# A new hand-written order of issue for the attention block of a fused attention, RWKV and convolution kernel

## Chip, cores and metric

The kernel runs on one core of one Trainium2 chip. The metric is the device time of one execution in microseconds (us), the median of three runs. The core has TensorE (matmul, with its weight loads), VectorE, ScalarE, GpSimd, and SyncE, which issues most DMAs; each engine works through its own instructions in program order.

## Reference

Batch 2, 12 heads, 448 tokens, 64 numbers per head. Causal attention is followed by two feed-forward blocks:

```
scores = q @ k.T / 8, masked above the diagonal;  attn = softmax(scores);  x = attn @ v      # to (2, 448, 768)
xk = mu_k*x + (1-mu_k)*x_prev;  xr = mu_r*x + (1-mu_r)*x_prev                                # x_prev: one token earlier
r = sigmoid(xr @ w_r);  v = relu(xk @ w_k)**2 @ w_v;  x = r * v                              # w_r 768x768, w_k 768x1024
h = relu(x @ w_in);  gate = sigmoid(conv over 3 tokens of h);  out = (h * gate) @ w_out
```

The weights come as 64-bit floats and are turned into 32-bit ones on the chip.

## The kernel before, in words

Attention is cut into 12 **jobs**, one for each batch entry and pair of heads (job 6 to 11 are batch entry 1). The rows of a job's score matrix are cut into 7 tiles (0 to 6) of 64 tokens; tile i has 64·(i+1) columns, and both heads of the pair lie side by side on the 128 partitions. A job goes through these steps, which the program names by short words:

- `Lk`, `Lv`: DMA loads of q, k and v. `kqT`: TensorE transposes q and k; `kC.k`, `kC.q`: the copies out of PSUM.
- `sc.1`, `sc.2`: the score matmuls. `red.i`: VectorE adds the mask and takes the row maximum of tile i (L334). `exp.i`: ScalarE's exponential with its row sum (L343). `rec`: VectorE takes the reciprocals of the seven sums (L350, L351). `norm.i`: tile i is scaled in place (L71 on GpSimd, L73 on VectorE, L75 on ScalarE).
- `T.a` (tiles 6, 5, 0), `T.b` (tiles 4 to 1): TensorE transposes the scaled tiles. `C.aX`, `C.aY`, `C.bX`, `C.bY`: the four copies out of PSUM into the tile `pt`. `V.a`, `V.b`: the matmuls with v, into the tile `po`.
- `mP.1`, `mD.1`: the two passes that make xr of this pair of heads from `po`; `mP.0`, `mD.0` those for xk (L73 or L75, and L416). `mH`, `mL`: xr is split into a high and a low part for the three-matmul products (L82, L90); `mH`, `mL` of jobs 0 to 5 belong to batch entry 0.

Around the jobs stand steps of the first feed-forward block. `wN:L` loads a slice of weights (w0 to w5 are the six slices wr0 to wr5 of w_r, w6 to w8 the slices wk0 to wk2 of w_k); `a` (ScalarE), `b`, `c`, `d`, `e` turn it into 32-bit numbers (L136, L139, L141, L143, L145), and `h`, `l` split it into a high and a low part (L86, L90). `kN:H`, `kN:L` do the same for xk of job N. `prE.B.C` is one product step: three matmuls (L65 to L67) of weight slice E with chunk C (one pair of heads) of xr for batch entry B; so `pr4.1.0` is the first step that reads wr4. `srE.B` copies a finished sum out of PSUM. `E0` to `E3` are the first four sums with w_k, 18 matmuls each. `W*n` are matmuls on a constant that only keep TensorE at work.

All of these, on four engines, are issued in the order of one long string, `ORDER`, inside a scheduling region that keeps the order of issue on each engine as written. A token such as `8:norm.4/v` is job 8, step norm, tile 4, on VectorE; `/p` is GpSimd and `/a` ScalarE. So the string decides two things: where a step stands in its engine's queue, and, for the steps that more than one engine can do, which engine does it. PSUM banks and buffers go round in the order of the string too.

```
    with tc.manual_schedule(engines={ET.PE, ET.Activation, ET.DVE, ET.Pool}):
        for token in ORDER.split():
            issue(token)
```

Behind the string comes the rest of the program (the other sums with w_k, then w_v, w_in and w_out), whose order a scheduler sets. Its first TensorE instruction is the first matmul with wk2.

Of the kernel before, what the change touches and what calls it, by code (L numbers as in the profile page):

```python
# [19 lines left out]
def kernel(  # L20
# [451 lines left out]
    class Slice:  # L472
# [27 lines left out]
        3:kC.q/a 1:exp.5 0:C.bX/a 2:red.2 0:norm.5/p 1:rec 0:C.bY/a 1:norm.6/p 2:exp.2 2:red.1 0:T.a 1:norm.0/p  # L500
        2:exp.1 1:norm.5/p 0:C.aX/v 0:C.aY/v 2:red.0 1:norm.1/p 1:norm.4/p W*1 4:kqT 2:exp.6 4:kC.q/v 3:sc.2 2:exp.4
        2:exp.3 2:red.5 2:exp.0 W*1 1:T.a 3:red.3 0:V.a 5:Lk 1:norm.2/p Wend 2:exp.5 2:Lv 1:C.aX/v 3:red.2
        1:norm.3/p 4:kC.k/a 3:red.0 3:red.5 3:sc.1 2:rec 1:C.aY/v 2:norm.5/p 3:red.6 1:T.b 3:exp.0 3:red.4
        2:norm.0/p 3:exp.5 4:sc.2 3:red.1 3:exp.2 2:norm.6/p 6:Lk 4:red.3 0:V.b 1:C.bX/v 5:kqT w1:L 3:exp.3 3:exp.6
        2:norm.1/p 3:exp.4 4:red.2 1:C.bY/a 2:norm.4/p 2:norm.3/p 4:red.0 3:exp.1 4:red.5 2:T.a 2:C.aY/v 4:exp.0
        2:norm.2/p 5:kC.q/a 5:kC.k/a 2:T.b 3:Lv 2:C.aX/a 3:rec 0:mP.1/v 4:exp.5 3:norm.2/p 4:sc.1 4:exp.2 4:exp.3
        2:C.bX/v 3:norm.5/p 6:kqT 4:red.6 3:norm.1/p 5:sc.2 4:red.4 4:red.1 2:C.bY/v 4:exp.6 6:kC.k/a 2:V.a
        3:norm.4/p 4:exp.1 4:exp.4 0:mP.0/v 5:red.0 3:norm.3/p 5:red.3 w1:a 5:red.2 2:V.b 6:kC.q/v 3:T.b 3:norm.6/p
        7:Lk 3:norm.0/p 5:red.5 4:rec 3:T.a 3:C.bY/v w1:b/p 3:C.bX/a 4:norm.4/p 5:sc.1 1:Lv 2:mP.1/a 5:exp.0
        3:C.aX/v 2:mP.0/a 0:mD.1 5:red.1 5:red.6 4:norm.2/p 3:C.aY/a 0:mD.0 4:norm.3/p 3:V.b 5:exp.2 8:Lk 4:norm.5/p  # L510
        5:exp.3 6:sc.2 5:exp.1 4:norm.1/p 2:mD.1 4:norm.6/p 5:exp.5 5:red.4 7:kqT 7:kC.k/a 4:Lv 3:V.a 6:red.0 2:mD.0
        2:mH/p 4:norm.0/p 7:kC.q/v 3:mP.1/v 4:T.b 5:exp.6 9:Lk w1:c 0:mH/p 5:exp.4 5:rec 4:T.a 4:C.aX/a w1:d 1:V.a
        1:V.b 0:mL/p 6:exp.0 5:Lv 4:C.bX/a 3:mP.0/a 5:norm.5/p 5:norm.6/p 6:sc.1 6:red.5 6:red.3 4:C.bY/a 5:norm.0/p
        7:sc.1 4:C.aY/a 6:red.2 5:T.a 3:mD.1 6:exp.5 6:red.4 6:exp.2 6:red.1 6:red.6 4:V.a 7:red.1 6:exp.4 6:exp.3
        6:exp.1 6:exp.6 4:V.b 3:mD.0 5:C.aY/v 7:red.4 7:red.6 5:C.aX/a 8:kqT w2:L 1:mP.1/a 5:norm.3/p 6:rec
        5:norm.4/p 8:kC.k/a w1:e 2:mL/p 5:norm.2/p 6:Lv 5:norm.1/p 3:mH/p 5:T.b 8:kC.q/a 5:C.bY/a 7:sc.2 3:mL/p
        9:kqT w1:h 5:V.a 4:mP.1/v 1:mP.0/a 5:C.bX/v 7:red.2 9:kC.k/v 7:red.0 6:norm.3/p 7:exp.2 10:Lk 1:mD.1 7:exp.0
        6:norm.1/p 9:kC.q/a 5:V.b 7:red.3 6:norm.2/p 6:norm.4/p 7:exp.1 6:T.b 7:red.5 7:exp.3 w1:l/p 1:mD.0 1:mH/p
        6:norm.0/p 1:mL/p 6:C.bX/a 9:sc.1 4:mP.0/a 6:C.bY/v 9:red.6 8:sc.2 8:sc.1 6:norm.6/p 7:exp.4 4:mD.1 8:red.2
        6:norm.5/p w2:a 7:exp.6 8:red.3 11:Lk pr1.0.0 8:Lv pr1.0.1 4:mD.0 5:mP.1/v 7:exp.5 8:exp.3 w2:b/p 8:red.6  # L520
        7:rec 4:mH/p 8:red.1 5:mP.0/v 6:T.a 6:C.aY/a pr1.0.2 8:red.5 pr1.0.3 10:kqT 6:C.aX/a 8:exp.2 5:mD.1 6:V.a
        8:exp.6 8:red.0 6:V.b w2:c 8:exp.5 8:red.4 8:exp.1 7:norm.2/p 7:norm.0/p 10:kC.q/a 5:mD.0 10:kC.k/a 9:sc.2
        9:red.4 7:norm.6/p 9:red.1 8:exp.4 7:norm.3/p 11:kqT 7:norm.1/p 4:mL/v 8:exp.0 7:norm.4/p 7:T.b 5:mH/p w2:d
        5:mL/p 8:rec 7:norm.5/p 11:kC.q/v pr1.0.4 9:red.3 6:mP.1/a pr1.0.5 7:C.bY/a 8:norm.1/p 8:norm.3/p 6:mP.0/a
        9:red.2 11:kC.k/a 7:T.a 10:sc.1 sr1.0/v 7:C.bX/a w2:e 9:exp.4 8:norm.6/p 9:red.0 7:C.aX/a 7:C.aY/v 9:exp.2
        8:norm.2/p w2:h 10:sc.2 10:red.6 9:exp.0 9:exp.1 7:Lv w3:L 8:norm.0/p 9:exp.3 6:mD.1 7:V.b 9:red.5 9:exp.6
        7:V.a 8:norm.4/p 8:norm.5/p 10:red.5 10:red.0 9:exp.5 w3:a 10:Lv 6:mD.0 10:red.4 9:rec 8:T.b 7:mP.1/v 8:T.a
        w2:l/p 8:C.aX/a 8:C.bY/a w3:b/v 6:mH/p 10:exp.4 10:exp.0 8:C.aY/a pr2.0.0 7:mP.0/a 10:exp.5 9:norm.4/v w3:c
        10:red.3 9:norm.3/p pr2.0.1 pr2.0.2 pr2.0.3 10:red.2 pr2.0.4 w3:d 9:norm.0/p 8:C.bX/a pr2.0.5 11:sc.2
        10:red.1 7:mD.1 10:exp.6 w3:e 9:norm.5/p 11:red.5 7:mD.0 6:mL/p 11:Lv 10:exp.1 9:norm.2/v 11:sc.1 11:red.6  # L530
        9:Lv w3:h 8:V.b 9:norm.6/p 10:exp.3 8:V.a 11:red.2 sr2.0/a 9:T.a 11:red.3 w0:L 10:exp.2 8:mP.1/v 10:rec
        11:red.0 11:exp.6 w5:L 11:exp.0 9:norm.1/p w3:l/p 11:red.4 10:norm.3/v 9:T.b 11:exp.4 11:red.1 9:C.aY/v
        10:norm.0/p 11:exp.5 8:mP.0/v 11:exp.3 10:norm.1/p 10:norm.6/p pr2.1.0 9:C.bX/v pr3.0.0 pr3.0.1 10:norm.5/p
        9:C.aX/v 11:exp.2 11:exp.1 9:C.bY/a 7:mH/p pr3.0.2 11:rec pr3.0.3 10:norm.2/v 8:mD.1 11:norm.3/v 10:norm.4/p
        pr3.0.4 pr3.0.5 8:mD.0 w0:a 11:norm.5/a 10:T.a 10:T.b 10:C.aX/a 9:V.a 9:V.b w0:b/p 10:C.bY/v 11:norm.2/a
        11:norm.4/a 10:C.bX/v 11:norm.1/v 11:T.b 11:norm.6/p 11:norm.0/p 11:T.a 10:C.aY/a 11:C.bX/a w0:c w5:a
        11:C.bY/a 7:mL/p 9:mP.1/v 10:V.b 11:C.aX/a 10:V.a 9:mP.0/v 11:C.aY/a 9:mD.1 11:V.b 8:mH/p w0:d w5:b/v w0:e
        10:mP.1/a 11:V.a pr1.1.0 9:mH/a 10:mP.0/a pr3.1.0 8:mL/p 11:mP.1/v w0:h w0:l/p w5:c pr3.1.1 act2 10:mD.1
        w4:L 11:mP.0/a 11:mD.1 pr3.1.2 pr1.1.1 9:mD.0 pr0.0.0 9:mL/p 11:mH/p w5:d k5:H/p 10:mH/a pr0.0.1 w4:a
# [248 lines left out]
```

## Time and profile before

| | us |
|---|---|
| median of 3 runs | 365.78 (365.63 to 366.27) |
| the profiled execution, its own time | 365.75 |
| span of that execution, first to last instruction | 364.0 |
| TensorE busy in the span | 354.6 (97%) |
| VectorE busy | 289.0 (79%) |
| ScalarE busy | 222.1 (61%) |
| GpSimd busy | 112.0 (31%) |

Times below are us from the start of the span. A busy share is an average over stages with different limits, and a matmul counts as busy while it is in the pipeline, so the stages have to be looked at one by one. TensorE's granted clock is 1.00, the upper of its two levels (2.4 GHz), in every stretch of the rows below.

### The profile page before, as it was taken

What the parts mean: (1) busy time and instruction counts of PE and PEld (TensorE: products, weight loads), DVE (VectorE), ACT (ScalarE), POOL (GpSimd) and SP (SyncE); (2) the same over time, 40 slices, a digit from 0 to 9 for tenths busy, and PEclk for the clock granted to TensorE, in tenths of its full rate; (3) what the DMA queues carried; (4) which work ended last, traced back from release to release, by engine and by line L of the source; (5) the groups of instructions that cost most, each with busy time, mean ns of one, the idle gap of its engine ahead of it and who ended that gap; (6) DMA issues with size and microseconds to landing.
All of it is one profiled execution on the core that took longest, in us unless ns stands there. A gap on an engine that the chain in (4) does not pass through costs nothing.

```text
span 364.0 us, 7204 instructions
## 1 busy us (share of the span) xinstructions
PE 354.6 (97%) x2724; PEld 316.8 (87%) x2724; DVE 289.0 (79%) x551; ACT 222.1 (61%) x474; POOL 112.0 (31%) x168
## 2 busy tenths in 40 slices
...
GB/s 128 150 134 209 131 210 198 43 163 2 89 86 128 55 165 175 143 145 204 184 135 121 157 127 173 133 140 162 86 89 97 76 3 0 2 60 92 62 48 44
DMA packets 60351, 41.39 MB, mean 114 GB/s; under 512 B 34424, under 2 KB 59292, under 8 KB 60316
## 3 DMA queue, kind: packets, MB, share of 16 engines
...
q8 instruction: 21, 0.34, 0.4%
...
HBM read 38.17 MB, written 2.75 MB: 112 GB/s over the span
## 4 chain that ended last, share of the span: by engine, by line
PE 81%; DVE 16%; issue 2%; POOL 0%; ACT 0%; ACTq 0%; POOLq 0%
PE pk L66 5%; PE pk L67 5%; PE pout L67 5%; PE pk L65 5%; PE ph L67 5%; PE ph L66 5%; PE pout L66 5%; PE pout L65 5%; PE pv L66 5%; PE pv L67 5%; PE ph L65 5%; PE pv L65 5%; DVE e L334 5%; PE pr L65 3%; PE pr L66 3%; PE pr L67 3%
## 5 line engine op out<-in xcount | busy, mean ns | idle before, releaser
L724 POOL TENSOR_TENSOR cv<-cv,hT 128x448 f32<-128x448 f32 x16 | 23.2, 1454 | 153.1 <-ACT cv L723 153.1
L71 POOL TENSOR_SCALAR p<-p,st 128x64 f32<-128x64 f32 (+6 forms) x75 | 39.5, 548 | 20.5 <-ACT p L343 10.6
L343 ACT ACTIVATE p<-e,st 128x448 f32<-128x448 f32 (+6 forms) x84 | 42.0, 504 | 5.0 <-DVE st L334 4.7
L334 DVE CUSTOM_DVE_ANT_0 e<-s,mask 128x256 f32<-128x256 f32 (+6 forms) x84 | 31.8, 414 | 0.7 <-PE s L321 0.7
L753 ACT ACTIVATE osb<-pout 128x384 f32<-128x384 f32 x14 | 6.9, 492 | 40.9 <-PE pout L67 39.8
L391 PE MATMUL po<-pt,v 128*64 128x128 f32 (+4 forms) x384 | 24.2, 277 | 0.6 <-PE Ya L363 0.3
L321 PE MATMUL s<-kT,qT 64*64 64x64 f32 (+6 forms) x336 | 23.4, 388 | 0.4 <-DVE small L139 0.2
L391 PEld LDWEIGHTS po<-pt,v 128*64 128x64 f32 x384 | 20.3, 137 | 3.9 <-ACT p L343 0.5
L321 PEld LDWEIGHTS s<-kT,qT 64*64 64x64 f32 x336 | 14.7, 132 | 7.2 <-ACT qT L78 0.6
L65 PE MATMUL pout<-wo_t,g 128*128 128x384 f32 x49 | 16.4, 334 | 0.0
L66 PE MATMUL pout<-wo_t,g 128*128 128x384 f32 x49 | 16.4, 334 | 0.0
L67 PE MATMUL pout<-wo_t,g 128*128 128x384 f32 x49 | 16.4, 334 | 0.0
L343 ACT ACTIVATION_READ_ACCUMULATOR p<-e,st 128x1 f32 x84 | 16.1, 192 | 0.0
L65 PE MATMUL pout<-wo_u,g 128*128 128x384 f32 x42 | 14.0, 334 | 0.0
L66 PE MATMUL pout<-wo_u,g 128*128 128x384 f32 x42 | 14.0, 334 | 0.0
L67 PE MATMUL pout<-wo_u,g 128*128 128x384 f32 x42 | 14.0, 334 | 0.0
L720 DVE SCALAR_TENSOR_TENSOR cv<-hT,cw,cv 128x448 f32<-128x448 f32 x16 | 13.7, 855 | 0.1
L86 ACT ACTIVATE g<-cv 128x448 fp32r<-128x448 f32 x16 | 9.2, 576 | 7.1 <-POOL cv L724 7.0
L90 DVE TENSOR_TENSOR g<-cv,g 128x448 fp32r<-128x448 f32 x16 | 12.1, 755 | 1.8 <-ACT g L86 1.8
L719 DVE SCALAR_TENSOR_TENSOR cv<-hT,cw,cv 128x448 f32<-128x448 f32 x16 | 12.9, 810 | 0.0
L718 ACT ACTIVATE cv<-hT,cw 128x448 f32<-128x448 f32 x16 | 10.6, 670 | 2.3 <-DVE g L90 2.1
L90 POOL TENSOR_TENSOR xr<-m,xr 128x448 fp32r<-128x448 f32 x9 | 11.3, 1257 | 0.3
...
## 6 DMA issues: line engine op xcount, KB each, us to landing
rqk<-in_q_dram SPq DMA_DIRECT2D x24, 112.0 KB, 3.0
...
rqk<-in_k_dram SPq DMA_DIRECT2D x22, 112.0 KB, 2.9
...
```

What stands on the lines that cost most here:

```text
L65: nc.tensor.matmul(ps_out, lh, rh, start=first, stop=False)
L66: nc.tensor.matmul(ps_out, lh, rl, start=False, stop=False)
L67: nc.tensor.matmul(ps_out, ll, rh, start=False, stop=last)
L71: nc.gpsimd.tensor_scalar(out_, in_, s, 1.0, ALU.mult, ALU.mult)
L90: e.tensor_tensor(out_, x, f32(h), ALU.subtract)
L321: nc.tensor.matmul(held[self.name(f"s{f}")][1][h, o:z], qT[r, i * LO:(i + 1) * LO], kT[r, :(i + 1) * LO], start=True, stop=True,)
L334: nc.vector.tensor_tensor_reduce(t[:, :w], used(self.name(f"s{f}"))[:, o:z], mask[:, S - w:], -SCALE, 3e38, ALU.add, ALU.min, self.st[:, 0 ...
L343: nc.scalar.activation(p[:, :w], self.s[i][:, :w], AF.Exp, bias=self.st[:, 0, i:i + 1], scale=-1.0, accum_out=self.st[:, 1, i:i + 1],)
L391: nc.tensor.matmul(self.T["po"][j * D:(j + 1) * D, 1 + i * LO - z:1 + (i + n) * LO], self.v[:, kc, j], self.T["pt"][:, a - z:a + n * LO], ...
L719: nc.vector.scalar_tensor_tensor(a, hc, cw[:, NF + f:NF + f + 1], a, ALU.mult, ALU.add)
L720: nc.vector.scalar_tensor_tensor(a, hT[:, 2:S + 2], cw[:, 2 * NF + f:2 * NF + f + 1], a, ALU.mult, ALU.add)
L724: nc.gpsimd.tensor_tensor(a, a, hc, ALU.mult)
```

## The change

The string `ORDER` is replaced by another one. Nothing else differs. Of its 716 tokens 712 remain: the four that go are `W*n` tokens, of which there are now three fewer matmuls (14 instead of 17). All the other steps are there in both, in other places, and some on another engine. Two lines of the table:

```diff
-        0:Lk sm:L 1:Lk sm:a W0 W*2 0:kqT 0:kC.k/v sm:n 0:kC.q/a W*2 0:sc.1 2:Lk W*1 1:kqT 0:red.1 0:exp.1 0:red.4
+        0:Lk W0 sm:L W*2 0:kqT 0:kC.k/a sm:a 1:Lk 0:kC.q/v W*2 0:sc.2 W*1 1:kqT sm:n 0:red.0 0:red.5 0:red.2 0:red.3
```

Steps on each engine in the string, before and after: VectorE 220 and 223, ScalarE 175 and 183, GpSimd 115 and 104. The largest moves between engines are in `kC` (9 and 11 on VectorE), `C` (19 on VectorE in both), `mH` (10 and 7 on GpSimd), `norm` (75 and 70 on GpSimd), `kN:L` (6 and 3 on GpSimd), `l` of the weight slices (5 and 3 on GpSimd) and `b` (4 and 6 on GpSimd).

The first place is VectorE's queue behind the last `rec`, that of job 11. Before, from the last pass over a tile `p` (`norm.1` of job 11) on; `wr0c` and `wr5c` are slices being turned into 32-bit numbers, `m` and `mixed` the passes that make xr and xk:

```order
L73 TENSOR_SCALAR p_1_120<-p_1_120,st 128x128
L141 TENSOR_SCALAR wr0c<-wr0c 128x768
L73 TENSOR_SCALAR m_1904<-po_1836,mu 128x448
L73 TENSOR_SCALAR mixed<-po_1836,mu 128x448
L416 SCALAR_TENSOR_TENSOR m_1904<-po_1836,mu,m_1904 128x448
L143 SCALAR_TENSOR_TENSOR wr0c<-wr0raw,wr0c 128x768
L139 TENSOR_SCALAR wr5c<-wr5c 128x768
L145 SCALAR_TENSOR_TENSOR wr0c<-wr0raw,wr0c 128x768
```

and now, from the same pass on:

```order
L73 TENSOR_SCALAR p_1_120<-p_1_120,st 128x128
L78 COPY pt_135<-Xb_1829 128x512
L78 COPY pt_135<-Xa_1811 128x512
L78 COPY pt_136<-Xb_1876 128x512
L78 COPY pt_136<-Ya_1900 128x512
L78 COPY pt_136<-Yb_1877 128x512
L141 TENSOR_SCALAR wr4c<-wr4c 128x768
L416 SCALAR_TENSOR_TENSOR m_1917<-po_1855,mu,m_1917 128x448
L143 SCALAR_TENSOR_TENSOR wr4c<-wr4raw,wr4c 128x768
```

Slice wr0 has moved ahead of this place, three of the four last copies into `pt` have come to VectorE from ScalarE, and wr4 follows directly.

The second place is the end of the same queue's work on wr4. Before, the passes ahead of the low part of wr4 (`wr4hl`) were:

```order
L139 TENSOR_SCALAR wr4c<-wr4c 128x768
L141 TENSOR_SCALAR wr4c<-wr4c 128x768
L145 SCALAR_TENSOR_TENSOR wr5c<-wr5raw,wr5c 128x768
L416 SCALAR_TENSOR_TENSOR mixed<-po_1927,mu,mixed 128x448
L143 SCALAR_TENSOR_TENSOR wr4c<-wr4raw,wr4c 128x768
L90 TENSOR_TENSOR wr5hl<-wr5c,wr5hl 128x768
L145 SCALAR_TENSOR_TENSOR wr4c<-wr4raw,wr4c 128x768
L416 SCALAR_TENSOR_TENSOR mixed<-po_1906,mu,mixed 128x448
L78 COPY sr_2098<-pr_0_1764 128x448
L90 TENSOR_TENSOR wr4hl<-wr4c,wr4hl 128x768
```

and now:

```order
L139 TENSOR_SCALAR wr5c<-wr5c 128x768
L145 SCALAR_TENSOR_TENSOR wr4c<-wr4raw,wr4c 128x768
L90 TENSOR_TENSOR xr_105<-m_1982,xr_105 128x448
L416 SCALAR_TENSOR_TENSOR mixed<-po_1945,mu,mixed 128x448
L416 SCALAR_TENSOR_TENSOR mixed<-po_1924,mu,mixed 128x448
L90 TENSOR_TENSOR xr_106<-m_1971,xr_106 128x448
L141 TENSOR_SCALAR wr5c<-wr5c 128x768
L90 TENSOR_TENSOR xk_2002<-mixed,xk_2002 128x448
L143 SCALAR_TENSOR_TENSOR wr5c<-wr5raw,wr5c 128x768
L90 TENSOR_TENSOR wr4hl<-wr4c,wr4hl 128x768
```

The low part of wr4 now stands ahead of that of wr5 instead of behind it, and the `L90` passes of jobs 10 and 11 (`xr_105`, `xr_106`), which stood further ahead, are now among these rows.

The third place is TensorE's queue where it first reads wr4. Before, the rows ahead of it (one `xr` per pair of heads, 101 to 106) were:

```order
L65 MATMUL pr_1_2087<-xr_102,wr5hl 128x448
L66 MATMUL pr_1_2087<-xr_102,wr5hl 128x448
L67 MATMUL pr_1_2087<-xr_102,wr5hl 128x448
L65 MATMUL pr_1_2038<-xr_104,wr0hl 128x448
L66 MATMUL pr_1_2038<-xr_104,wr0hl 128x448
L67 MATMUL pr_1_2038<-xr_104,wr0hl 128x448
L65 MATMUL pr_1_2112<-xr_101,wr4hl 128x448
L66 MATMUL pr_1_2112<-xr_101,wr4hl 128x448
```

and now:

```order
L65 MATMUL pr_1_2014<-xr_102,wr3hl 128x448
L66 MATMUL pr_1_2014<-xr_102,wr3hl 128x448
L67 MATMUL pr_1_2014<-xr_102,wr3hl 128x448
L65 MATMUL pr_1_1991<-xr_106,wr2hl 128x448
L66 MATMUL pr_1_1991<-xr_106,wr2hl 128x448
L67 MATMUL pr_1_1991<-xr_106,wr2hl 128x448
L65 MATMUL pr_1_2079<-xr_101,wr4hl 128x448
L66 MATMUL pr_1_2079<-xr_101,wr4hl 128x448
```

Of the 72 product steps, 19 stood ahead of the last `V` (that of job 11) and 22 do now. The first step with wr4 was the 30th behind that `V` and is now the 21st; the first with wr5 was the 25th and is now the 30th.

## Rows read from the trace of the kernel before

**Rows 1.** By stretch: length, busy us of PE, PEld, DVE, ACT, POOL; clock, DMA.

```profile
8.00:94.50 86.50, 82.50 (x1321) 66.47 (x1317) 85.04 (x274) 77.74 (x235) 61.36 (x98) 1.00 0.54 133
94.50:112.50 18.00, 18.00 (x91) 16.34 (x88) 16.77 (x20) 8.85 (x15) 14.59 (x11) 1.00 0.34 107
112.50:142.40 29.90, 29.90 (x147) 27.15 (x146) 26.93 (x34) 12.57 (x19) 8.46 (x6) 1.00 0.39 124
142.40:360.00 217.60, 217.60 (x1127) 201.29 (x1126) 158.75 (x219) 120.32 (x203) 24.71 (x29) 1.00 0.32 106
```

**Rows 2.** The chain that ended last, early and around job 11: start, us, what.

```profile
8.11 0.42 PE W L556 x2
...
85.45 0.20 DVE st L351
...
87.29 1.20 DVE pt L78 x2
88.49 1.10 DVE p L73
...
90.94 3.67 PE po L391 x64
94.61 0.40 PE pr L65
```

**Rows 3.** TensorE in order of time: start, us, operation, out<-in.

```profile
112.00 0.37 PE L65 MATMUL pr<-xr,wr0hl 128*128 128x448 f32 x1
...
112.62 0.37 PE L65 MATMUL pr<-xr,wr4hl 128*128 128x448 f32 x1
...
127.50 0.37 PE L65 MATMUL pk<-xk,wk0hl 128*128 128x448 f32 x1
...
142.38 0.40 PE L65 MATMUL pk<-xk,wk2hl 128*128 128x512 f32 x1
```

**Rows 4.** GpSimd in order of time, three of its passes (two in one row).

```profile
88.37 1.13 POOL L90 TENSOR_TENSOR xr<-m,xr 128x448 fp32r<-128x448 f32 x1
...
106.92 3.77 POOL L90 TENSOR_TENSOR xk<-mixed,xk 128x448 fp32r<-128x448 f32 x2
```

**Rows 5.** VectorE's groups by shape, 0 to 86 us: busy us, mean ns of one.

```profile
L350 DVE TENSOR_SCALAR st<-st 128x7 f32<-128x7 f32 x12 | 3.5, 288 | 0.0
...
L73 DVE TENSOR_SCALAR p<-p,st 128x192 f32<-128x192 f32 x2 | 2.2, 1084 | 0.0
...
L143 DVE SCALAR_TENSOR_TENSOR wr3c<-wr3raw,wr3c 128x768 int32<-128x768 int32 x1 | 1.8, 1766 | 0.0
...
L73 DVE TENSOR_SCALAR p<-p,st 128x320 f32<-128x320 f32 x1 | 0.4, 439 | 0.0
```

**Rows 6.** VectorE in order of time behind job 11's last scaled tile.

```profile
85.27 0.15 DVE L350 TENSOR_SCALAR st<-st 128x7 f32<-128x7 f32 x1
...
93.01 0.55 DVE L139 TENSOR_SCALAR wr5c<-wr5c 128x768 f32<-128x768 f32 x1
93.48 0.96 DVE L145 SCALAR_TENSOR_TENSOR wr0c<-wr0raw,wr0c 128x768 int32<-128x768 int32 x1
94.73 0.68 DVE L73 TENSOR_SCALAR m<-po,mu 128x448 f32<-128x448 f32 x1 [0.29 <-PE po L391]
...
97.57 0.95 DVE L143 SCALAR_TENSOR_TENSOR wr5c<-wr5raw,wr5c 128x768 int32<-128x768 int32 x1
98.44 1.58 DVE L90 TENSOR_TENSOR xr<-m,xr 128x448 fp32r<-128x448 f32 x1
100.48 0.97 DVE L90 TENSOR_TENSOR xr<-m,xr 128x448 fp32r<-128x448 f32 x1 [0.46 <-POOL xr L82]
...
103.04 1.90 DVE L145 SCALAR_TENSOR_TENSOR wr5c<-wr5raw,wr5c 128x768 int32<-128x768 int32 x1
...
106.88 0.96 DVE L90 TENSOR_TENSOR wr5hl<-wr5c,wr5hl 128x768 fp32r<-128x768 f32 x1 [0.47 <-ACT wr5hl L86]
...
110.71 0.94 DVE L90 TENSOR_TENSOR wr4hl<-wr4c,wr4hl 128x768 fp32r<-128x768 f32 x1
```

More of the change, by code (lines that the diff above doesn't have):

```diff
@@ L500 @@
[L500 to L539, printed above, removed]
@@ new lines @@
+        2:kqT 1:red.5 1:red.2 2:kC.k/v 1:red.0 0:exp.6 1:red.3 3:Lk 1:sc.1 2:kC.q/a 0:Lv 0:rec sm:T 2:sc.2 1:exp.2
+        1:exp.5 0:norm.2/p 1:red.1 1:red.4 3:kqT 1:exp.1 1:exp.0 0:norm.4/p 1:exp.3 sm:C 0:norm.1/p 1:red.6 3:kC.q/v
+        1:exp.6 0:norm.3/p 1:exp.4 2:red.0 W*2 0:T.b 0:norm.0/p 4:Lk 2:red.5 0:norm.6/p 2:red.2 2:red.3 0:C.bY/a
+        3:kC.k/a 2:sc.1 0:norm.5/p 0:C.bX/v 0:T.a 1:rec 2:red.6 1:norm.6/p 2:exp.3 3:sc.1 0:C.aX/a 2:exp.2 2:exp.5
+        2:red.1 1:norm.0/p 3:sc.2 0:C.aY/v 4:kqT 1:norm.2/p 3:red.6 1:norm.5/p 2:exp.0 2:red.4 1:norm.4/p 2:exp.1
@@ new lines @@
+        1:norm.1/p 1:T.a 3:red.5 Wend 4:kC.k/v 3:red.0 w1:L 1:C.aY/v 2:exp.4 1:Lv 2:exp.6 1:norm.3/p 2:rec 3:exp.0
+        0:V.b 1:T.b 4:kC.q/a 3:exp.6 2:norm.5/p 2:norm.1/p 4:sc.1 3:red.1 2:norm.3/p 3:exp.5 0:V.a 3:red.3 1:C.bY/v
+        2:norm.6/p w1:a 2:norm.0/p 2:norm.2/p w1:b/p 3:red.2 3:red.4 1:C.bX/v 1:C.aX/v 4:red.4 3:exp.3 2:norm.4/p
+        0:mP.1/a 5:Lk 3:exp.4 4:red.1 2:T.a 3:exp.2 4:sc.2 2:T.b 3:exp.1 0:mP.0/v 2:C.aX/a 4:red.6 2:C.aY/a 3:rec
+        w1:c 3:norm.3/p 3:norm.0/p 5:kqT 4:exp.1 4:red.3 4:red.0 2:C.bX/v 4:exp.4 5:kC.k/v 0:mD.1 3:norm.5/p
@@ new lines @@
+        3:norm.1/p 4:red.2 1:V.a 5:kC.q/a 4:exp.0 1:V.b 5:sc.2 4:exp.3 4:red.5 4:exp.6 3:norm.2/p 3:norm.6/p 6:Lk
+        0:mD.0 3:norm.4/p 5:red.0 0:mH/p 2:Lv 0:mL/p 6:kqT 5:red.2 2:C.bY/a 5:red.3 4:exp.5 5:red.5 7:Lk 3:Lv
+        6:kC.q/a 3:T.a 4:exp.2 3:T.b 5:sc.1 3:C.aY/v w1:d 4:rec 6:kC.k/a 3:C.aX/a 3:C.bY/a 1:mP.1/a 4:norm.4/p
+        4:norm.1/p 5:red.1 4:norm.3/p 4:norm.6/p 3:C.bX/a 5:exp.0 6:sc.2 w1:e 1:mP.0/v 5:exp.1 2:V.a 5:red.4 5:Lv
+        5:red.6 5:exp.3 7:kqT 5:exp.5 4:norm.5/p 2:V.b 4:norm.2/p 4:norm.0/p 7:kC.q/a 6:sc.1 4:Lv 5:exp.2 1:mD.1
```

50 lines of the change are left out of this document (37 added, 13 removed).

## The prediction

> **What bounds the kernel now.** I read busy time by stretch first [rows 1]. From 94.5 us on TensorE is busy for the whole of each stretch (18.00 of 18.00, 29.90 of 29.90, 217.60 of 217.60): everything behind the last `V` of job 11 is a queue of matmuls without a hole, and its end is its start plus its length. Up to 94.5 us VectorE is the full one (85.04 of 86.50), ScalarE next (77.74), and TensorE has holes. The chain that ended last says the same [rows 2]: up to 89.6 us it runs over VectorE, pass after pass, then through job 11's transposes and 3.67 us of `V` matmuls, and from 94.61 on over TensorE's products alone. So the time is set by two things: when the last `V` is through, and how many product steps are still to do then, as long as no step finds its operands late.
>
> TensorE's prices are plain [rows 3]. A product step takes 112.62 - 112.00 = 0.62 us. The four `E` sums take 142.38 - 127.50 = 14.88. From the last `V`'s end at 90.94 + 3.67 = 94.61 [rows 2] on: 53 steps × 0.62 + 14.88 = 47.74, which gives 142.35 against 142.38 in the trace for the first matmul with wk2, where the string ends. Behind that the program is the same, and VectorE is busy for only 158.75 of 217.60 us [rows 1], so I let a shift at 142.38 go through to the end one to one.
>
> The second thing to see is how near the products run to their weights. The low part of wr4 is done at 110.71 + 0.94 = 111.65 [rows 6] and first read at 112.62 [rows 3], 0.97 later. VectorE has little to spare there, and some of its passes are drawn out: the same L145 pass takes 0.96 once and 1.90 another time, and L90 on `xr` 0.97 and 1.58 [rows 6]. These are passes with both ends in SBUF. One case shows what does it: a pass over `p` on VectorE stands at 88.49 for 1.10 us and ends at 89.59 [rows 2], though a wider one takes 0.44 [rows 5]; GpSimd's pass of 1.13 us that began at 88.37 ended at 89.50 [rows 4], and the VectorE pass ended just behind it. Below I call this a block. The Trainium skill (SBUF — State Buffer, section on the two separate sides) has a rule for it: VectorE and GpSimd share a port pair that one instruction holds for its whole length, and the other waits. By that rule a pass that goes from GpSimd to VectorE doesn't stop being blocked, which is against hoping for much here, and the trace agrees in this case.
>
> **The change part by part.** I price an unblocked VectorE pass by the distance to the next start: 0.60 for a pass out of PSUM (1.20 for two [rows 2]), 0.54 for the copies of q and k, 0.47 for L139 and L141 (93.01 to 93.48), 0.87 for L143 and L145 (97.57 to 98.44), 0.90 for L90 [rows 6], about 0.35 for a `norm` (a row of 0.44, less some 0.08 of overlap with the next [rows 5]). 0.53 for `kN:L` is an estimate: the 0.90 of L90 on 768 columns, scaled to 448.
>
> *Up to job 11's `rec`.* VectorE has 164 steps of the string up to there before and 167 now. More: 2 `kC` (+1.1), `c`, `d`, `e` of wr0 (0.47 + 0.87 + 0.87 = +2.2), `l` of wr3 (+0.9), 3 `norm` (+1.0). Fewer: 3 `C` (-1.8), 1 `mP` (-0.6), 1 `mL` (-0.9), 1 `b` (-0.5). Sum +1.4. Job 11's `rec` ended at 85.65 [rows 2], so it ends at 87.05 if blocks and waits ahead of it stay as they are. What those come to now: two `norm` passes over 192 columns of 1.08 mean, where 320 columns took 0.44, so no less than 0.65 each (1.3), wr3's L143 of 1.77 instead of 0.95 (0.8), twelve L350 of 0.288 mean where an unblocked one takes 0.15 (1.7) [rows 5, 6], so some 3.8 us.
>
> *From `rec` to the last `V`.* Behind `rec` VectorE now has 2 `mP`, 1 `mD`, 1 narrow `norm` (0.2) and five copies into `pt`: 8 × 0.60 + 0.2 = 5.0, so the last copy ends at 92.05. Job 11's two `V` halves follow it; four halves take 3.67 [rows 2], two take 1.84. The last `V` ends at 93.9 instead of 94.6. Before, the same way went 3.9 us from `rec` to the last `norm`, then through transposes, ScalarE's copies and four `V` halves.
>
> *TensorE behind it.* 22 product steps are done by then instead of 19, so 50 remain: 50 × 0.62 + 14.88 = 45.88. The string ends at 139.8 without any stall, 2.6 earlier than 142.38. The three missing `W*n` matmuls I count at nothing: they stand in the first stretch, where VectorE's passes set the pace and TensorE has holes; on the path they would be worth 3 × 0.42 = 1.3 us (a row of two records is one such matmul) [rows 2].
>
> *The wait it may run into.* wr4 is now read first at step 21: 93.9 + 20 × 0.62 = 106.3, 6.3 earlier than before. VectorE's work from 92.05 to the end of `w4:l`: 8 passes `mP` or `mD` (4.8), `c`, `d`, `e`, `l` of wr4 (0.47 + 0.87 + 0.87 + 0.90), `b`, `c`, `d` of wr5 (0.47 + 0.47 + 0.87), two `mL` (1.8), one `kN:L` (0.5): 12.0, so 104.05 with nothing in the way, and 2.25 us of cover. What can be in the way: `w4:c` waits for GpSimd's `w4:b`, which stands behind the `mL` of jobs 7 and 8 (1.13 each [rows 4], the first not before `mD.1` of job 7 at 88.9): 0.45 us. And blocks: before, from 89.59 to 111.65, 22.06 us held 17.1 of such passes at the prices above, so 5.0 were lost, 1.2 of it in three waits (0.29, 0.46, 0.47 [rows 6]) and 3.8 in blocks on 15 passes with both ends in SBUF, 0.25 each. The stretch now has 10 such passes: 2.5. Bounds: nothing at all (no stall), and all of the 5.0 (2.75 us of stall). I take 0.45 + 2.5 = 2.95, less the cover of 2.25: a stall of 0.7. It is the middle way since GpSimd, too, has fewer steps (115 to 104) but its longest ones, two-input passes of up to 1.9 (3.77 for two [rows 4]), are still there.
>
> The other operands come in time by the same count: `mL` of job 11 ends at some 101.5 to 103 and is read at step 14 (102.0), a tie that the stall at step 21 covers; `w5:l` needs 2.8 us more VectorE work than `w4:l` and is read 5.6 later; the wk1 slice, the tightest of the later ones, has 17.6 us of passes behind `w4:l`, near 130 with 0.25 on each of 23 blockable ones, and is read near 133.
>
> **Sum.** -2.6 + 0.7 = -1.9, on the profiled execution's own 365.75, which is the median's 365.78 within the spread: 363.9.
>
> **Rivals.**
>
> *Slower: wr4 comes too late.* The change brings the wr4 products forward by more than VectorE's work on them: 30 steps and four sums (33.5 us) stand behind the first of them, where 24 steps and four sums (29.8) did. The point that decides: `w4:l` at 108.8 gives the old 142.38. I expect 107.0. If the blocks there cost the old 5.0 and the 1.4 us more work up to `rec` brings blocks of 1 us with it, `w4:l` is at 110.05, TensorE stands still for 2.7 us in front of its first wr4 product, the string ends at 143.5 and the time is 366.9. For it: the old margin was only 0.97. Against it: five blockable passes fewer in this stretch.
>
> *No change that can be told.* What the measurement tells from no change is about 0.2%, 0.73 us. Blocks and waits at wr4 cost the old 5.0 and nothing else moves: `w4:l` at 109.05, string end 142.5, 365.9. Or ScalarE takes VectorE's place: its 77.74 busy us of 86.5 leave 8.8, and it gets seven more steps ahead of job 11's `rec` (two `mH`, four `norm`, one slice's `a` and `h`, less one net copy), some 4 us at about 0.55 each; if half of it delays `exp` and `rec`, the last `V` is 2 us later and the gain is gone.
>
> *More than I forecast: the blocks ahead of `rec` go.* These are some 3.8 us [rows 5, 6], and order alone could part the passes that collide. If half of them go, `rec`, the last `V` and `w4:l` all move 2 us ahead: 361.9. Against it: the new string still has as many blockable passes there, 12 `rec` and six `norm` among them.
>
> **How the numbers follow.** Forecast (a gain of 0.75 to 3 us) 0.43, 363.9; more than that 0.17, 361.9; no change 0.18, 365.9; slower 0.22, 366.9. Faster by over 0.2% is the first two, 0.60; within it 0.18; slower 0.22. The range goes from 361.5 to 367.0: the low end takes in half of the blocks ahead of `rec`, the high one the slower rival's price, and about a tenth is left out on each side. The likeliest case by itself, with the stall between 0 and 1.9, goes from 363.1 to 365.0.
>
> **What would show it.** Right: the first product step behind the last `V` near 93.9, with 22 steps ahead of it; a hole of up to 2 us on TensorE in front of its first wr4 product, or `w4:l` just ahead of it; first wk2 matmul near 140.5; from there to the end the same length as before (364.0 - 142.38 = 221.6). Wrong: job 11's `rec` later than 88 or with waits for ScalarE in VectorE's rows; the hole at wr4 over 2.6 us; any hole behind the first wk2 matmul; or a stretch up to `rec` in which the drawn-out L350, L73 and L143 rows are gone, which would be the larger gain.

## The result, and the profile after

The changed kernel takes 360.13 us (359.91 to 362.15) where the kernel before took 365.95 (365.63 to 366.27) in the same comparison: a ratio of 0.985, 95% interval 0.982 to 0.989. The gain is 5.8 us, three times the 1.9 that I forecast, and 360.13 lies below the range.

The stretches of the profiled execution after (span 358.1 us, own time 359.91), as in [rows 1] but cut where this execution has its last `V` and its first wk2 matmul:

```profile
8.00:94.50 86.50, 85.57 (x1345) 70.69 (x1338) 84.15 (x283) 82.55 (x247) 61.53 (x97) 1.00 0.57 142
8.00:90.50 82.50, 81.57 (x1326) 67.05 (x1318) 80.26 (x277) 79.72 (x241) 58.10 (x93) 1.00 0.59 149
90.50:136.50 46.00, 46.00 (x226) 41.80 (x223) 40.85 (x58) 21.91 (x36) 11.30 (x11) 1.00 0.32 103
136.50:354.00 217.50, 217.50 (x1126) 201.21 (x1125) 158.22 (x220) 119.64 (x201) 24.41 (x29) 1.00 0.33 107
```

The first row has the same bounds as in [rows 1]: GpSimd is as busy as before (61.53 and 61.36), VectorE a little less (84.15 and 85.04), ScalarE more (82.55 and 77.74). The full engines ahead of the last `V` are now VectorE (80.26 of 82.50) and, close behind, ScalarE (79.72). TensorE counts as busy for 81.57 of it and waits for others only twice, 0.2 us each, where it waited for 3.3 us in all up to 94 us before; whether it sets the pace there is tried below with four product steps. From 90.5 us on TensorE is busy for the whole of each stretch, as it was from 94.5.

TensorE in order of time, answering to [rows 3]: the first product step behind the last `V`, the first with wr4, the first `E` sum, the first matmul with wk2:

```profile
90.53 0.47 PE L65 MATMUL pr<-xr,wr0hl 128*128 128x448 f32 x1
...
102.82 0.37 PE L67 MATMUL pr<-xr,wr2hl 128*128 128x448 f32 x1
103.03 0.37 PE L65 MATMUL pr<-xr,wr4hl 128*128 128x448 f32 x1
...
121.01 0.37 PE L65 MATMUL pk<-xk,wk0hl 128*128 128x448 f32 x1
...
136.51 0.40 PE L65 MATMUL pk<-xk,wk2hl 128*128 128x512 f32 x1
```

The wr4 matmul starts 0.21 behind the one ahead of it, the pace of the queue: no stall there. From 136.51 to the end of the span are 221.6 us, as from 142.38 before.

VectorE's groups by shape, 0 to 84 us, answering to [rows 5]:

```profile
L350 DVE TENSOR_SCALAR st<-st 128x7 f32<-128x7 f32 x12 | 2.0, 168 | 0.2 <-ACT p L343 0.2
L73 DVE TENSOR_SCALAR p<-p,st 128x320 f32<-128x320 f32 x3 | 1.7, 579 | 0.0
...
L143 DVE SCALAR_TENSOR_TENSOR wr3c<-wr3raw,wr3c 128x768 int32<-128x768 int32 x1 | 0.9, 947 | 0.0
```

The drawn-out rows of [rows 5] are gone: L350 has a mean of 168 ns instead of 288, wr3's L143 takes 947 instead of 1766, and no tile of 192 columns is left on VectorE. Smaller ones have come: three tiles of 320 columns have a mean of 579, where one took 439.

VectorE in order of time from job 11's `rec` on, answering to [rows 6]:

```profile
83.02 0.20 DVE L351 RECIPROCAL st<-st 128x7 f32<-128x7 f32 x1
...
87.69 0.68 DVE L78 COPY pt<-Yb 128x512 f32<-128x512 f32 x1
89.36 0.56 DVE L141 TENSOR_SCALAR wr4c<-wr4c 128x768 int32<-128x768 int32 x1 [0.99 <-POOL wr4c L139]
...
94.92 0.95 DVE L145 SCALAR_TENSOR_TENSOR wr4c<-wr4raw,wr4c 128x768 int32<-128x768 int32 x1
...
100.39 0.96 DVE L90 TENSOR_TENSOR wr4hl<-wr4c,wr4hl 128x768 fp32r<-128x768 f32 x1
```

`rec` ends at 83.22 (85.65 before), and the low part of wr4 at 101.35, 1.7 us ahead of its first use. Not one of the passes on wr4 is drawn out.

To see the blocks as one number I added up, over VectorE's passes, the distance from each start to the next, less the price of the same pass unblocked (priced as in the prediction) and less the waits. Ahead of job 11's `rec` that makes 5.5 us of blocks before and 2.1 after; from the last copy into `pt` to the end of `w4:l`, 3.9 before (counted from the last scaled tile) and 0.6 after. Below, "blocks" is this number. It hangs on the prices: with the lower quartile of the same pass over all the traces as its price, the blocks ahead of `rec` are 6.4 before and 2.4 after. So the fall, 3.4 to 4.0, is surer than either number.

GpSimd's busy time up to `rec`, before and after:

```profile
8.00:85.60 77.60, 56.61 (x92) 1.00 0.60 148
```

```profile
8.00:83.20 75.20, 52.80 (x86) 1.00 0.65 163
```

That is 73% and 70% of the stretch, with nine two-input passes (L90) before and ten after; and VectorE has 31 passes with both ends in SBUF there (the small weights left out) where it had 26. Neither GpSimd's load nor the number of passes that could be blocked explains that the blocks fell by more than half.

### The profile page after: what moved, and what is told of

Its sections match the earlier page's. It is cut to its first block, busy times and chain, and to the rows that moved or that the text cites. A ratio compares the mean times of both kernels' runs of the same rounds, so it can differ in the third digit from the quotient of the medians.

```text
span 358.1 us, 7189 instructions
## 1 busy us (share of the span) xinstructions
PE 351.9 (98%) x2718; PEld 316.0 (88%) x2718; DVE 280.6 (78%) x554; ACT 223.8 (62%) x482; POOL 96.7 (27%) x157
## 4 chain that ended last, share of the span: by engine, by line
PE 94%; ACT 2%; DVE 2%; POOL 1%; issue 0%; POOLq 0%; ACTq 0%
PE po L391 6%; PE pk L66 5%; PE pk L67 5%; PE pout L66 5%; PE pk L65 5%; PE ph L66 5%; PE ph L67 5%; PE pout L67 5%; PE pout L65 5%; PE pv L67 5%; PE pv L66 5%; PE ph L65 5%; PE pv L65 5%; PE pr L65 5%; PE pr L66 4%; PE pr L67 4%
## 5 line engine op out<-in xcount | busy, mean ns | idle before, releaser
L71 POOL TENSOR_SCALAR p<-p,st 128x64 f32<-128x64 f32 (+6 forms) x70 | 34.6, 513 | 21.8 <-DVE st L334 12.4
L334 DVE CUSTOM_DVE_ANT_0 e<-s,mask 128x192 f32<-128x192 f32 (+6 forms) x84 | 31.6, 415 | 0.4 <-ACT p L343 0.2
L321 PE MATMUL s<-kT,qT 64*64 64x384 f32 (+6 forms) x336 | 22.1, 387 | 0.5 <-DVE kT L78 0.2
L90 DVE TENSOR_TENSOR g<-cv,g 128x448 fp32r<-128x448 f32 x16 | 12.1, 757 | 1.8 <-ACT g L86 1.8
L718 DVE SCALAR_TENSOR_TENSOR cv<-hT,cw,cv 128x448 f32<-128x448 f32 x16 | 12.9, 812 | 0.0
L90 POOL TENSOR_TENSOR xr<-m,xr 128x448 fp32r<-128x448 f32 x10 | 12.0, 1196 | 2.1 <-ACT xr L86 1.7
```

Of the source, the lines that this page charges most:

```text
L71: nc.gpsimd.tensor_scalar(out_, in_, s, 1.0, ALU.mult, ALU.mult)
L90: e.tensor_tensor(out_, x, f32(h), ALU.subtract)
L321: nc.tensor.matmul(held[self.name(f"s{f}")][1][h, o:z], qT[r, i * LO:(i + 1) * LO], kT[r, :(i + 1) * LO], start=True, stop=True,)
L334: nc.vector.tensor_tensor_reduce(t[:, :w], used(self.name(f"s{f}"))[:, o:z], mask[:, S - w:], -SCALE, 3e38, ALU.add, ALU.min, self.st[:, 0 ...
L718: nc.vector.scalar_tensor_tensor(a, hc, cw[:, NF + f:NF + f + 1], a, ALU.mult, ALU.add)
```

## The experiments

Each ran beside the kernel before on the same chip; ratios and intervals are against that.

**Places or engines.** The change moves steps and gives 98 of the 712 to another engine. One kernel has the new string with each step on its old engine:

```diff
-        0:Lk W0 sm:L W*2 0:kqT 0:kC.k/a sm:a 1:Lk 0:kC.q/v W*2 0:sc.2 W*1 1:kqT sm:n 0:red.0 0:red.5 0:red.2 0:red.3
+        0:Lk W0 sm:L W*2 0:kqT 0:kC.k/v sm:a 1:Lk 0:kC.q/a W*2 0:sc.2 W*1 1:kqT sm:n 0:red.0 0:red.5 0:red.2 0:red.3
...
```

> The new order of the steps, but every step on the engine that it had before. Theory (blocks: VectorE's passes with both ends in SBUF stand still while GpSimd works, and the new string parts the two): what stands beside what is upset again, blocks ahead of job 11's rec go from 2 us back to 4 to 6, time 363 to 366 us. Rival 1 (the share of work: GpSimd has fewer steps): the gain is lost, 365 to 366. Rival 2 (the order alone: 22 product steps instead of 19 ahead of the last V, a shorter way from rec to V): the gain stays, 360 to 361.

The other has the old string with each step on its new engine:

```diff
-        0:Lk sm:L 1:Lk sm:a W0 W*2 0:kqT 0:kC.k/v sm:n 0:kC.q/a W*2 0:sc.1 2:Lk W*1 1:kqT 0:red.1 0:exp.1 0:red.4
+        0:Lk sm:L 1:Lk sm:a W0 W*2 0:kqT 0:kC.k/a sm:n 0:kC.q/v W*2 0:sc.1 2:Lk W*1 1:kqT 0:red.1 0:exp.1 0:red.4
...
```

> The old order of the steps, but every step on the engine that it has in the new string. Theory (blocks): no better than before, since the places were not made for these engines, 364 to 367 us, blocks ahead of job 11's rec 4 to 6 us. Rival 1 (the share of work): the gain is there, 360 to 362. Rival 2 (the order alone): 366.

Measured: 372.83 us (ratio 1.014, 1.008 to 1.019) and 380.89 (1.035, 1.029 to 1.041). Both are slower than either kernel, more than I expected of any case. VectorE's longest waits between 12 and 96 us, first in the one with the new places, then in the one with the new engines (engine, line, waited for: us in all, times, longest):

```profile
DVE e L334 <- ACT p L343: 2.1, 3, 0.9
DVE sr L78 <- PE pr L67: 1.4, 1, 1.4
```

```profile
DVE st L350 <- ACT p L343: 3.2, 2, 2.9
DVE mixed L73 <- ACT m L75: 2.3, 1, 2.3
```

The kernel after has one wait of 1.0 and two of 0.2 in such a stretch. `rec` of job 11 ends at about 94 us in both. The blocks ahead of it are 6.9 with the new places alone and 5.4 with the new engines alone, where they were 5.5 before; the waits in the stretch come to 5.1 and 8.1. In the second kernel TensorE's granted clock is also 0.72, so partly at its lower level, between 88 and 94 us and between 109 and 115, each time just behind a wait of TensorE (2.48 and 1.63 us). So neither half alone takes the blocks away, and what each alone is worth can't be read from such halves: each is a schedule out of step with itself.

**Front or tail.** The string is cut behind job 11's last `V`. One kernel has the new string up to there and the remaining steps in the old order:

```diff
 ... 11:V.b 11:C.aX/a 11:V.a
-act2 11:mP.1/a 9:mD.1 pr0.1.0 pr0.1.1 w4:d ...
+7:mD.0 pr2.1.0 pr3.0.4 pr3.0.5 9:mD.1 w5:b/v ...
```

> The new string up to the last V of job 11, behind it the steps that are left in the old string's order. Theory (most of the gain is the time at which the last V ends, 90.5 instead of 94.5 us, with 22 product steps done): 360 to 362 us, as long as wr4 and wr5 come in time. Rival (the tail behind the last V, where blocks up to wr4's low part fell from 4 to 0.8 us, is needed too): a hole on TensorE ahead of a wr4 or wr5 product, 362.5 to 364.

Measured: 360.62 us (360.51 to 361.08; ratio 0.981, 0.974 to 0.987). The front alone brings all of the gain but some 0.5 us, which is less than the new string's own runs lie apart (359.91 to 362.15). The last `V` is through at 91.20, TensorE has a small wait of 0.4 us ahead of wr4, and the first wk2 matmul starts at 137.34. The blocks ahead of `rec` are 2.1, as in the kernel after.

The other has the old string up to the last `V` and the remaining steps in the new order:

```diff
 ... w0:e 10:mP.1/a 11:V.a
-pr1.1.0 9:mH/a 10:mP.0/a pr3.1.0 8:mL/p 11:mP.1/v ...
+w0:h w0:l/p pr0.0.0 pr0.0.1 pr0.0.2 pr0.0.3 pr0.0.4 w4:L ...
```

> The old string up to the last V of job 11, behind it the steps that are left in the new string's order. Theory (the gain is made ahead of the last V): 365 to 367 us, the last V ends at 94.5 as before. Rival (the tail brings part of it): 362 to 364.

Measured: 373.84 us (1.015, 1.009 to 1.022), which neither case had. In the profiled execution the front, the same steps as in the kernel before, is itself 3 us late: TensorE waited 1.91 us up to 30.94, its granted clock was 0.72 between 30 and 36 us, and `rec` ends at 88.60 instead of 85.65. The rest is lost behind the last `V`. VectorE's row there, ScalarE's and SyncE's load of wr4:

```profile
106.02 0.56 DVE L141 TENSOR_SCALAR wr4c<-wr4c 128x768 int32<-128x768 int32 x1 [8.65 <-POOL wr4c L139]
```

```profile
103.74 0.54 ACT L78 COPY sr<-pr 128x448 f32<-128x448 f32 x1 [5.49 <-PE pr L67]
```

```profile
97.44 0.37 SPq L158 DMA_DIRECT2D wr4raw<-in_moe_w_r_dram  x1
```

VectorE stood still for 8.65 us, for two reasons. The load of wr4 was issued only at 97.44: there are two buffers for raw slices, and the old front leaves them with wr0 and wr5 until then. A load of this size lands some 4 us later (4.1 for wr5's in this run). And ScalarE began on wr4 only at 104.17: in the new tail the copy `sr0.0` stands ahead of it in ScalarE's queue, and waited 5.49 us for the last product with wr0. In the kernel after the load is issued at 76.35, in the one before at 94.51:

```profile
76.35 0.50 SPq L158 DMA_DIRECT2D wr4raw<-in_moe_w_r_dram  x1
```

```profile
94.51 0.37 SPq L158 DMA_DIRECT2D wr4raw<-in_moe_w_r_dram  x1
```

So this run doesn't tell what the new tail is worth on the old front. It shows what I had passed over: the new string takes wr0 out of the way early, so that wr4 can be loaded 18 us sooner, and its tail counts on that.

**Two blocked passes out of the kernel before.** Two `norm` passes of VectorE that collide with GpSimd (`norm.2` of job 9, drawn out by 1.6 us, and `norm.1` of job 11, by 0.9) go to GpSimd's own queue; all else is as before:

```diff
- ... 10:exp.1 9:norm.2/v 11:sc.1 ... 10:C.bX/v 11:norm.1/v 11:T.b ...
+ ... 10:exp.1 9:norm.2/p 11:sc.1 ... 10:C.bX/v 11:norm.1/p 11:T.b ...
```

> The old string with two tokens changed: norm.2 of job 9 and norm.1 of job 11 go from VectorE to GpSimd. They are the two longest blocks ahead of the last V (1.8 us and 1.1 us for passes that take 0.2 to 0.3 unblocked). Theory (blocks cost what they last): VectorE gets to job 11's rec 1.5 us earlier and has nothing to wait for at norm.1, the time falls by 1 to 2.5 us, to 363.5 to 365. Rival (the time of a blocked pass is hidden, the chain goes through GpSimd or ScalarE): 365.5 to 366.5, no change.

Measured over six runs: 363.11 us (ratio 0.990, 0.988 to 0.993), a gain of 3.1, a little more than expected. Rows of VectorE behind 82 us:

```profile
82.88 0.20 DVE L351 RECIPROCAL st<-st 128x7 f32<-128x7 f32 x1
...
88.33 1.92 DVE L143 SCALAR_TENSOR_TENSOR wr0c<-wr0raw,wr0c 128x768 int32<-128x768 int32 x1
```

`rec` ends at 83.08 instead of 85.65, the blocks ahead of it are 3.4 instead of 5.5, and the last `V` is through at 91.23 instead of 94.54. The two blocks were worth 1.63 + 0.94 = 2.57 us and the bare passes 0.34, together 2.9: the time follows VectorE's queue nearly one to one. Two tokens of the 716 give over half of what the whole new string gives. Blocks behind `rec` stay (L143 at 88.33 takes 1.92).

**More GpSimd passes on the new string.** Six passes that nothing needs (two SBUF inputs, 128x448, as wide as the `mL` passes) are put on GpSimd behind `k6:H`, `k3:H` and `k7:L`, on a tile that is filled once:

```diff
+            nc.gpsimd.memset(spare[0], 1.0)
...
+        elif what == "zp":
+            nc.gpsimd.tensor_tensor(spare[0][:, 0, :448], spare[0][:, 1, :448], spare[0][:, 2, :448], ALU.add)
...
- ... k6:H/p w4:h ... k3:H/p k5:H/a ... k7:L/p pr0.1.5 ...
+ ... k6:H/p zp zp w4:h ... k3:H/p zp zp k5:H/a ... k7:L/p zp zp pr0.1.5 ...
```

> The new string with six added GpSimd passes (two inputs in SBUF, 128x448, results unused) in GpSimd's gaps behind the last V, at about 94, 98 and 103 us. Nothing waits for them but GpSimd's own later steps. Theory (blocks): VectorE's L143, L145, L90 passes beside them are drawn out by 0.3 to 1 us each, w4:l ends at 103 to 105 instead of 101.35, a hole of 0 to 2 us on TensorE ahead of the first wr4 product (103.03), time 360 to 362. Rival (GpSimd's gaps are of no use to VectorE): w4:l stays within 0.3 of 101.35, 360.1.

A second kernel has the same passes with 8 columns:

```diff
-            nc.gpsimd.tensor_tensor(spare[0][:, 0, :448], spare[0][:, 1, :448], spare[0][:, 2, :448], ALU.add)
+            nc.gpsimd.tensor_tensor(spare[0][:, 0, :8], spare[0][:, 1, :8], spare[0][:, 2, :8], ALU.add)
```

> As the run with six added GpSimd passes, but of 8 columns instead of 448: as many added instructions, nearly no time in SBUF. Both theories: w4:l within 0.3 us of 101.35, 360.1 us. If it is slower all the same, the cost of the six passes is in their issue and not in blocks.

Measured: 364.80 us over six runs (0.996, 0.994 to 0.998) with the wide ones, 4.7 more than the new string without them, and 360.46 (0.983, 0.980 to 0.986) with the thin ones, no difference to it. VectorE with the wide ones, then GpSimd, in order of time:

```profile
95.30 1.20 DVE L139 TENSOR_SCALAR wr5c<-wr5c 128x768 f32<-128x768 f32 x1
96.42 1.90 DVE L145 SCALAR_TENSOR_TENSOR wr4c<-wr4raw,wr4c 128x768 int32<-128x768 int32 x1
...
104.74 1.89 DVE L90 TENSOR_TENSOR wr4hl<-wr4c,wr4hl 128x768 fp32r<-128x768 f32 x1
```

```profile
94.92 2.59 POOL L603 TENSOR_TENSOR spare<-spare 128x448 f32<-128x448 f32 x2
...
101.05 2.96 POOL L603 TENSOR_TENSOR spare<-spare 128x448 f32<-128x448 f32 x2
103.96 1.86 POOL L90 TENSOR_TENSOR xk<-mixed,xk 128x448 fp32r<-128x448 f32 x1
```

and TensorE's longest waits for others behind the last `V`:

```profile
PE pr L66 <- DVE xr L90: 1.5, 2, 0.9
PE pr L67 <- DVE wr4hl L90: 1.2, 1, 1.2
PE pr L65 <- ACT sr L78: 1.1, 1, 1.1
```

The last `V` is where it was (90.43), but VectorE's passes beside the spare ones take 1.90 instead of 0.95; the low part of wr4 ends at 104.74 + 1.89 = 106.63 instead of 101.35. Its slack of 1.7 is used up and TensorE gets holes, 3.8 us of the 4.0 by which this execution (363.89) is longer than that of the kernel after: the slower rival of the prediction, brought about on purpose. I had expected less, as that slack should have swallowed more.

**The price by itself.** A kernel that computes nothing of the reference has six passes of VectorE alone, then beside GpSimd passes with two SBUF inputs, then beside GpSimd passes with one, all on tiles of their own:

```diff
+        for g in (None, g_two, g_scale):
+            for v, n in ((v_scale, 6), (v_two, 6), (v_psum, 6), (v_thin, 3)):
+                if g:
+                    g(n)
+                v()
+                meet()
```

> No attention and no feed-forward: the output is zeros. VectorE's kinds of pass, six of each, measured alone, beside GpSimd passes with two inputs, and beside GpSimd passes with one: a scaling from SBUF to SBUF (384 columns, as norm), a difference of two SBUF tiles (448, as mL), a scaling out of PSUM (448, as mP), a thin pass (7 columns, as rec). Theory (blocks): out of PSUM 0.67 us in all three; the others alone 0.3 to 0.5, 0.6 and 0.15, and up to 1.2 us (the length of one GpSimd pass) longer beside GpSimd. Rival (GpSimd slows every VectorE pass a little, a matter of bandwidth): all kinds longer by the same share, the PSUM one too.

VectorE in order of time, six passes to a row: four rows alone, four beside two-input passes, four beside one-input passes (six GpSimd passes in each case, three beside the passes of 7 columns):

```profile
13.31 2.06 DVE L62 TENSOR_SCALAR vo<-a,col 128x384 f32<-128x384 f32 x6
...
15.98 3.29 DVE L66 TENSOR_TENSOR vo<-a,b 128x448 f32<-128x448 f32 x6
...
19.88 3.63 DVE L70 TENSOR_SCALAR vo<-pz,col 128x448 f32<-128x448 f32 x6
...
24.11 0.52 DVE L74 TENSOR_SCALAR vo<-a 128x7 f32<-128x7 f32 x6
...
25.24 7.20 DVE L62 TENSOR_SCALAR vo<-a,col 128x384 f32<-128x384 f32 x6
...
33.05 8.79 DVE L66 TENSOR_TENSOR vo<-a,b 128x448 f32<-128x448 f32 x6
...
42.44 3.63 DVE L70 TENSOR_SCALAR vo<-pz,col 128x448 f32<-128x448 f32 x6
...
49.08 3.39 DVE L74 TENSOR_SCALAR vo<-a 128x7 f32<-128x7 f32 x6
...
53.07 4.26 DVE L62 TENSOR_SCALAR vo<-a,col 128x384 f32<-128x384 f32 x6
...
58.28 4.37 DVE L66 TENSOR_TENSOR vo<-a,b 128x448 f32<-128x448 f32 x6
...
64.53 3.63 DVE L70 TENSOR_SCALAR vo<-pz,col 128x448 f32<-128x448 f32 x6
...
68.78 1.29 DVE L74 TENSOR_SCALAR vo<-a 128x7 f32<-128x7 f32 x6
```

A pass out of PSUM takes 3.63 / 6 = 0.61 in all three. A pass with both ends in SBUF loses (7.20 - 2.06) / 6 = 0.86 beside a two-input GpSimd pass, (8.79 - 3.29) / 6 = 0.92 if it has two inputs itself, and still 0.48 if it has only 7 columns; beside a one-input GpSimd pass the same three lose 0.37, 0.18 and 0.13. The Trainium skill (SBUF — State Buffer, section on the two separate sides) has an exclusive lock on a port pair that VectorE and GpSimd share; the trace agrees, and 3.63 three times is its other half, that a pass outside the lock is not touched.

**Four product steps moved behind the last `V`.** The new string does 22 product steps ahead of the last `V`; in this one it does 18:

```diff
- ... 11:exp.3 pr3.0.0 pr3.0.1 11:rec ... 10:norm.6/p pr3.0.2 sr0.0/a ... 7:mP.0/v pr3.0.3 10:norm.1/p ... k0:H/p pr3.0.4
+ ... 11:exp.3 11:rec ... 10:norm.6/p sr0.0/a ... 7:mP.0/v 10:norm.1/p ... k0:H/p pr3.0.0 pr3.0.1 pr3.0.2 pr3.0.3 pr3.0.4
```

> The new string with four product steps (the first four of wr3 for batch entry 0) moved from ahead of job 11's transposes to behind its last V: 18 steps instead of 22 ahead of it. Theory 1 (VectorE and the chain of job 11 set the last V, the steps fill holes of TensorE): the last V ends at 90.5 as before the move, four steps of 0.62 come on top, 362.6 us. Theory 2 (TensorE itself has become the bound ahead of the last V): the last V ends up to 2.5 us earlier and the time stays at 360.1.

Measured: 362.16 us (0.990, 0.987 to 0.992), 2.0 more than the new string; four steps are 4 × 0.62 = 2.5. The last `V` did not come sooner for it: it is through at 91.30 in the profile, 7.26 behind `rec` (7.31 in the kernel after); `rec` itself is 0.8 later there, after a wait of 0.88 for a load of k at 15 us. Where the steps stood TensorE has holes again, of 0.75, 0.28 and 0.52 us; the first:

```profile
81.88 0.27 PE L363 MATMUL Xa<-ident,p 64*128 64x64 f32 x1 [0.75 <-POOL p L71]
```

So the steps ahead of the last `V` lie in TensorE's holes and are a gain, and TensorE doesn't set that point by itself: with 22 steps it has no such hole left, and with 18 the point is no sooner.

**The new string without its `W*n` tokens.**

```diff
- ... 0:Lk W0 sm:L W*2 0:kqT ... 0:kC.q/v W*2 0:sc.2 W*1 1:kqT ... 2:red.0 W*2 0:T.b ...
+ ... 0:Lk W0 sm:L 0:kqT ... 0:kC.q/v 0:sc.2 1:kqT ... 2:red.0 0:T.b ...
```

> The new string without its four W*n tokens, seven matmuls on a constant of 0.42 us each in the first 20 us (the seven of W0 stay). Theory 1 (VectorE sets the pace): same time, 359.9 to 360.4 us. Theory 2 (TensorE has become the bound): 357.5 to 359.7. If the granted clock falls below 1.00 early on, it is slower and tells nothing of the two.

Measured: 360.41 us (0.985, 0.983 to 0.987): nothing that can be told from the new string. TensorE is busy for 80.31 of the 82.4 us up to its last `V`, and the granted clock is 1.00, the upper level, there too:

```profile
8.00:90.40 82.40, 80.31 (x1309) 66.04 (x1309) 79.90 (x275) 79.81 (x241) 58.19 (x93) 1.00 0.59 149
```

**The last two drawn-out `norm` passes of the new string**, put on GpSimd as in the fifth run:

```diff
- ... 7:norm.3/v 8:norm.4/v pr2.0.1 ... 6:mL/p 10:norm.4/v 11:exp.5 ...
+ ... 7:norm.3/v 8:norm.4/p pr2.0.1 ... 6:mL/p 10:norm.4/p 11:exp.5 ...
```

> The new string with norm.4 of jobs 8 and 10 on GpSimd instead of VectorE: the two largest blocks that are left ahead of the last V, 0.28 and 0.30 us on passes of 0.33. Theory (VectorE's work and blocks ahead of the last V come off the time one to one): 1.2 us less on VectorE, 358.9 to 359.6. Rival (GpSimd's own queue and job 10's transposes wait for the norm now, or TensorE is the bound): 359.9 to 360.6.

Measured: 360.11 us (0.984, 0.981 to 0.986), no change. The profiled execution took 361.21, the other three 359.60 to 360.23: in it TensorE waited 1.03 us for a load of k, up to 15.77, and its granted clock was 0.57, mostly the lower level, between 16 and 20 us. The waits of VectorE behind that have nothing to do with the edit. Between 60 and 86 us, where the moved passes stand, VectorE waits for 1.3 us, all of it for ScalarE, instead of 0.4, and its queue is 0.7 us shorter:

```profile
DVE st L350 <- ACT p L343: 0.6, 1, 0.6
DVE e L334 <- ACT p L343: 0.5, 2, 0.3
```

What gave 3.1 us in the kernel before gives nothing that can be told here. ScalarE (79.72 of 82.50) and TensorE (no wait over 0.2 us) are as full as VectorE by now; which of them takes the gain was not tried. No version was faster than the new string by more than the measurement can tell.

## Why the prediction was wrong, step by step

**What bounds the kernel: right.** The last `V` and a queue of products behind it set the time; the run with four later steps shows that TensorE alone is not the bound ahead of the last `V`, and the one without `W*n` that counting those matmuls at nothing was right. Behind the first wk2 matmul the program took its 221.6 us.

**Up to `rec`: this is the step that failed.** I had written of `rec`: "so it ends at 87.05 if blocks and waits ahead of it stay as they are." It ended at 83.22, 2.43 earlier than before, though VectorE had more to do: +1.4 by my prices. So blocks and waits ahead of it fell by 3.8; by the count above the blocks went from 5.5 to 2.1, and the waits fell by 0.2. One price was wrong, too: I took 0.90 for an `mL` from a row that was itself drawn out, where a two-input pass of 448 columns takes 3.29 / 6 = 0.55 when nothing is in the way (the pairs above). With that the added work is +1.8 and the fall 4.2.

I had priced the blocks (3.8 by the rows I chose, without the smaller ones), and then carried them over unchanged because the number of passes that could be blocked was no smaller. That is the wrong thing to count. GpSimd was busy for about the same share of this stretch, and VectorE had more passes in SBUF than before; what changed is which of them meet. The rival "more than I forecast" named this mechanism and let half of the blocks go for 2 us. I gave it 0.17; it was what happened, with 3.4 us at `rec`, and it reaches on to wr4. The last sign of being wrong that I named, that the drawn-out rows are gone, is the one that came.

That the blocks set the time is shown by the fifth run, where taking two of them out of the kernel before is worth 3.1 us, and by the sixth, where putting passes back on GpSimd costs 4.7. That it takes both, places and engines, to part them agrees with the first two runs, where the blocks stayed; but these are out of step in other ways as well, so it is not shown. Which pair of passes was parted by which move was not tried one by one.

**From `rec` to the last `V`: right in its length.** 7.31 us (83.22 to 90.53) against 6.85. The way is not quite the one that I drew: the last copy of VectorE ends at 88.37, and the four `V` halves of jobs 10 and 11 stand back to back on TensorE from 86.93 to 90.61.

**TensorE behind it: right.** 50 steps and the four `E` sums take 136.51 - 90.53 = 45.98, against 45.88, and 22 steps stood ahead.

**The stall at wr4: mis-sized.** I had 0.7; there was none. From the last copy into `pt` to the end of `w4:l` the wait for `w4:b` was 0.99 instead of 0.45, but the blocks were 0.6 instead of 2.5, and the two `mL` there took 0.7 less than I had priced them at. That makes 11.3 + 0.99 + 0.6 = 12.9, against 101.35 - 88.37 = 12.98 measured and 14.95 forecast. Here, too, I took the old loss per pass (0.25 each) over to a new order. And the early load of wr4 was not in my account at all: in the fourth run, without it, VectorE stood still for 8.65 us, though not for that alone.

The sum of it against the forecast: `rec` -3.83, `rec` to last `V` +0.46, TensorE +0.10, stall -0.70, together -3.97, from 363.9 to the profiled 359.9.
